# Chunked attention and a gated FFN on one core: heads paired as neighbours, one transfer per weight part, copied rows by a 32-bit or, and a new load order

## The chip, the cores and the metric

The kernel runs on one core of a Trainium2 chip. The metric is the device time of one execution in microseconds (us). Before the change its median is 240.51 us over 3 runs (240.17 to 240.85).

## The reference

Attention over chunks of 32 rows. Each chunk sees 16 rows to its left, itself, 8 rows to its right and 8 memory rows. Its output feeds an FFN with a relu gate. All inputs are f32, with B=4 batches, H=8 heads, S=768 rows and D=64.

```python
for c in range(S // 32):                      # 24 chunks
    l_start, r_end = max(0, 32 * c - 16), min(S, 32 * c + 32 + 8)
    k_full = concat([mem_k, k[:, :, l_start:r_end]], axis=2)      # 8 memory rows + up to 56
    v_full = concat([mem_v, v[:, :, l_start:r_end]], axis=2)
    scores = q[:, :, 32*c:32*c+32] @ k_full.T / sqrt(64)
    a = exp(scores - max(scores));  a = a / (sum(a) + 1e-9)
    out[:, :, 32*c:32*c+32] = a @ v_full
x = out.transpose(0, 2, 1, 3).reshape(3072, 512)
return (relu(x @ w_gate) * (x @ w_val)) @ w_out   # 512 -> 1536 -> 512
```

## The kernel before

**Tiles.** The 3072 tokens are 24 tiles of 128 rows (NT), six for each batch (TPB). A tile holds four chunks. Attention works tile by tile, and the FFN works on blocks of three or four tiles (BLOCKS).

**Attention of a tile.** GpSimd (POOL) loads Q and K with a cast to bf16: `qk_p` holds a pair of tiles (L218, the first six tiles), `qk_b` one tile (L209). TensorE (PE) transposes them into `qk_ps` (L229, L262). ACT or DVE copies the result to `qT` (`pair_q_copy`, L231) and `kT` (`pair_k_copy`, L235). `mem_keys` (L248) puts the transposed memory keys into `kT`, between each chunk's left context and the rest. `scores` (L297) computes 64 scores for each row and head. DVE takes the maximum (`mx`, L310), subtracts it (`dif`, L317), sums the exponents (L329), takes the reciprocal and multiplies (`p_n`, L340). ACT makes the exponents `p_exp` in three key ranges (L325). PE transposes `p_n` (`pT_ps`, L346), which is copied to `pT`. The products with V give `xT_ps` (L363), which is copied to `xT`, the input of the FFN. From tile 14 or 15 on the transposes are done by DMA.

**V.** `v_bd` has two buffers, used by the batches in turn. Each is a block diagonal of two heads: partitions 0 to 63 hold the 64 keys of one head, partitions 64 to 127 those of the other, each head with its own 64 columns. The two heads of a pair are h and h+4 (`HP * par + hp`). The eight memory rows of V must be in `v_bd`, and the off-diagonal part must be zero. For batch 0 both come from a pattern: `vmem_0` holds the memory rows of one chunk, and `pattern_spread` (L177) copies it over all 24 chunks on DVE. For later batches `mem_rows` (L155, its copies at L163) copies them from `vmem` on DVE. `load_v_rows` (L184, issued at L187) loads V itself: in batch 0 in halves of 12 chunks for each pair and parity, later in four loads for a batch. `zero` (L132) clears the second buffer by memset on POOL.

**FFN.** For each block and each of 12 column parts, four products with `w_gate_sb` (`g_ps`, L409), four with `w_val_sb` (`v_ps`, L409), a relu on ACT (`g_relu`, L415) and a multiplication on DVE (`gvT`, L421). The second matrix then takes 12 products for each tile (`out_ps`, L430), with a copy on ACT and a store by SyncE (SP). The gate and value weights come in five groups of columns (WB). Each group is four transfers: two matrices, by the two halves of 64 partitions (`load_gate_val`, L118).

**Order.** The kernel writes its own order. `op()` names a step with the engines that may do it, a cost, what it needs and a priority. `load()` names a POOL issue. `schedule()` runs a model of the engines with these costs: whenever an engine is free, it takes the first ready step by priority. The string LOADS is the order of POOL's issues: K0 and Q0 are pair loads, i the identity, v00 to v13 halves of V of batch 0 (half, pair), w0 to w4 groups of weights, z memsets of the second V buffer, k and q single tiles, o the halves of `w_out`, m the memory values, b the later batches of V. At most eight loads are in flight in the model. LEAD says how far the attention of a block runs ahead of the FFN. Until the first FFN product, PE fills time that it would wait with products on the identity (`idle_ps`, L401).

The order of the first products is by groups of columns over the early blocks, so that each group of weights is used by every early block before the next is needed:

```python
seq = [(blk, m) for g in range(WG) for blk in range(n_early) for m in range(WB[g], WB[g + 1])]
```

Of the kernel before, what the change touches and what calls it, by code (L numbers as in the profile page):

```python
# [12 lines left out]
BF16 = mybir.dt.bfloat16  # L13

# [6 lines left out]
def kernel(  # L21
# [20 lines left out]
    CH = 32  # L42
# [9 lines left out]
    BLOCKS = [3, 3, 4, 4, 3, 3, 4]  # L52
    LEAD = [21, 11, -1, 5, 8, 2, 14, 23]
# [4 lines left out]
    PAIRS = 3  # L58
    MEM_BY_SP = 0
# [3 lines left out]
    LOADS = """Q0 K0 K1 i Q1 K2 Q2 v00 z0 v02 v03 v01 w0 w1 v13 v11 v12 v10 w2 k8  # L63
               k10 w3 q7 k7 k6 q6 w4 q8 q9 k9 z3 o1 z2 z1 o0 m b1 k11 q16 q10
               k15 k12 k14 q11 k23 q21 q12 k16 q13 k13 q14 k20 q23 q15 k21 k19 b2 k17 k18 q17
               q20 q19 q18 q22 k22 b3"""
# [87 lines left out]

    def mem_rows(b, par, hp, eng):  # L155
        p = slice(64 * par, 64 * par + NMEM)
        src = vmem[p, b, HP * par + hp]
        i = bass.AP(tensor=src.tensor, offset=src.offset, ap=[src.ap[0], [0, NCH], [1, D]])
        o = v_bd[b % NSET][p, hp, :, D * par:D * par + D]
        if eng is nc.sync:  # L160
            eng.dma_start(o, i)
        else:
            eng.tensor_copy(o, i)  # L163

    def pattern_load():
        for par in range(2):
            p = 64 * par
            nc.sync.dma_start(
                vmem_f[p:p + NMEM, :, D * par:D * par + D],
                bass.AP(tensor=mem_v.tensor, offset=mem_v[0, HP * par, 0, 0].offset,  # L170
                        ap=[[D, NMEM], [NMEM * D, HP], [1, D]]))
# [12 lines left out]
    def load_v_rows(b, par, s0, s1, c0, c1):  # L184

        dst = v_bd[b % NSET].rearrange("p h c d -> p (h c) d")
        nc.gpsimd.dma_start(  # L187
            dst[64 * par + NMEM + s0:64 * par + NMEM + s1, c0:c1, D * par:D * par + D],
            bass.AP(tensor=v.tensor, offset=v[b, HP * par, 0, 0].offset + (CH * c0 + s0 - 16) * D,
                    ap=[[D, s1 - s0], [CH * D, c1 - c0], [1, D]]))  # L190

    def v_parts(b, par, c0, c1):
        parts = []
        if (b, par, c0) == (0, 0, 0):
            parts.append((b, par, 16, CTX, 0, 1))
            c0 = 1
        if (b, par, c1) == (B - 1, 1, HP * NCH):
            c1 -= 1
            parts.append((b, par, 0, 48, c1, c1 + 1))
        return parts + [(b, par, 0, CTX, c0, c1)]  # L200
# [34 lines left out]
    def pair_k_copy(r, j, eng):  # L235
        b, t = divmod(2 * r, TPB)
        ps = TMP["pair", r, 1]
        o = kT[b][:, :, 4 * t:4 * t + 8, :]
        copy(eng,
             bass.AP(tensor=o.tensor, offset=o.offset + j,  # L240
                     ap=[o.ap[0], [NCH * KW, HP], [KW, 8], [16 + NMEM, 2], [2, 8]]),
             ps[:, j].rearrange("p h (c x s) -> p h c x s", c=8, x=2))
# [5 lines left out]
    def mem_keys(b, eng):  # L248
        src = kmemT[:, b]
        copy(  # L250
            eng, kT[b][:, :, :, 16:16 + NMEM],
            bass.AP(tensor=src.tensor, offset=src.offset,
                    ap=[src.ap[0], [NMEM, HP], [0, NCH], [1, NMEM]]))
# [31 lines left out]
    def scores(a):  # L285
# [3 lines left out]
        for h2 in range(HP):  # L289
            m, par = h2 % 2, h2 // 2  # L290
            for g in range(4):
                c = 4 * t + g
                lo, hi = max(KW * c - 16, 0), min(KW * c + 48, NCH * KW)
                o0 = 64 * (2 * m + par) + lo - (KW * c - 16)
# [17 lines left out]
    def subtract(a):  # L312
# [146 lines left out]
    def psum(n):  # L459
# [9 lines left out]
       prio=(-8,), after=["warm"])  # L469
# [11 lines left out]
    for hp in range(HP):  # L481
        op(("spread", hp), {"DVE": 0.88}, lambda e, hp=hp: pattern_spread(hp), [("vm0", 0), ("vm0", 1)], prio=(-3 + 0.1 * hp,))
    for b in range(B):
        op(("kv", b), {"PE": 0.01}, lambda e, b=b: new_batch(b), take=["kv"],
           prio=(-5.5,) if b == 0 else (1, TPB * b - 2, 0), after=[("t", TPB * b - 2, 0)] if b else [])
        op(("new", b), {"ACT": 0.75}, lambda e, b=b: mem_keys(b, engine[e]), ["kmc", ("kv", b)],
           prio=(-4.5,) if b == 0 else (1, TPB * b - 2, 0))
# [9 lines left out]
    def keys_of(a):  # L497
        return ("tc", a - a % 2 + 1 if a < 2 * PAIRS else a, 1)

    for a in range(NT):  # L500
        b, t = divmod(a, TPB)
        last = t == TPB - 1
        for i in (1, 0):
            if a < 2 * PAIRS:
# [4 lines left out]
                if i:  # L509
                    for j in range(2):  # L510
                        op(("tc", a + j, i), {"ACT": 0.64, "DVE": 0.64}, lambda e, a=a, j=j: pair_k_copy(a // 2, j, engine[e]),
                           [("tc", a, i) if j else ("t", a, i)], (1, a - i, j), (), ["aps"] * j)
                else:
                    op(("tc", a, i), {"ACT": 1.2, "DVE": 1.22}, lambda e, a=a: pair_q_copy(a // 2, engine[e]), [("t", a, i)],
                       (1, a, 0), (), ["aps"])
# [14 lines left out]
           [("tc", a - a % 2 if a < 2 * PAIRS else a, 0), keys_of(a), ("new", b)] + ([] if last else [keys_of(a + 1)]), (1, a, 1), ["sps"],  # L530
           ["kv"] if last else [], ([("s", a - 1)] if a else []) + (pace(a) if a >= BY_DMA[0] else []))
# [16 lines left out]
        ready = [("vl", b, 0 if b else t // 3, n) for n in range(4 if b else 2 * HP)]  # L548
# [19 lines left out]
    for rank, (blk, m) in enumerate(seq):  # L568
        n = BLOCKS[blk]
        if m is not None:  # L570
            for w in range(2):
                op(("f", blk, m, w), {"PE": NFC * (0.0533 * n + 0.0025)}, lambda e, blk=blk, m=m, w=w: first(blk, m, w),
                   [("x", starts[blk] + i) for i in range(n)] + [("w", group_of[m], w, par) for par in range(2)],
# [26 lines left out]
    def load_qk_op(a, i):  # L600
        load(("qk", a, i), 1024, 1.05, lambda: load_qk(a, i), take=["qk"])

    def load_pair_op(r, i):
        load(("qk2", r, i), 1024, 1.66, lambda: load_pair(r, i), take=["pr"])

    def load_v_op(b, half, par, c0, c1, n, deps, after):
        for i, part in enumerate(reversed(v_parts(b, par, c0, c1))):
            rows = part[3] - part[2]
            load(("vl", b, half, n) if i == 0 else ("vx", b, n), rows * (part[5] - part[4]),
                 rows * (part[5] - part[4]) * 1.15e-3, lambda part=part: load_v_rows(*part), deps, (), after)  # L610

    def load_v_half(half, hps):
        c = NCH // 2
        for hp in hps:
            for par in range(2):
                load_v_op(0, half, par, NCH * hp + c * half, NCH * hp + c * half + c, 2 * hp + par, [("spread", hp)], [])

    def load_w_op(g):
        for w in range(2):
            for par in range(2):  # L620
                load(("w", g, w, par), 256, 0.1 + 0.31 * (WB[g + 1] - WB[g]), lambda g=g, w=w, par=par: load_gate_val(g, w, par))
# [4 lines left out]
    def load_batch(b):  # L626
        deps = [("z", x) for x in range(HP)] if b < NSET else [("v", TPB * (b - NSET + 1) - 1)]
        for par in range(2):
            for hp in range(HP):
                if b <= MEM_BY_SP:  # L630
                    op(("mr", b, par, hp), {"SP": 0.73}, lambda e, b=b, par=par, hp=hp: mem_rows(b, par, hp, nc.sync),
                       deps + [(("vm", par), 0.2)], (0, par, hp))
                else:
                    op(("mr", b, par, hp), {"DVE": 0.48}, lambda e, b=b, par=par, hp=hp: mem_rows(b, par, hp, nc.vector),
                       deps + [("vm", par)], (1.5,), (), (), [("s", TPB * b - MEM_LEAD[b])])
        c = HP * NCH // 2
        for par in range(2):
            for x in range(2):
                load_v_op(b, 0, par, c * x, c * x + c, 2 * par + x, [], deps)

    def load_by(name):
# [5 lines left out]
        elif what == "i":  # L647
            load("ident", 0, 0.55, lambda: make_identity(nc, ident_h))
        elif what == "v":
            load_v_half(n // 10, [n % 10])  # L650
# [9 lines left out]
        elif what == "b":  # L660
            load_batch(n)
# [11 lines left out]
    def holds_port(key):  # L673
        return key in ("kmb", "ib") or key[0] in ("vm0", "new", "spread", "mr") or (
            key[0] == "tc" and key[2] == 1 and key[1] >= BY_DMA[1])

    def schedule():
# [30 lines left out]
        while len(started) < len(ops) + len(loads):  # L708
# [8 lines left out]
            while moved:  # L717
                moved = False
                for e in ("POOL", "PE", "ACT", "DVE", "SP"):
                    if free[e] > t + 1e-9:  # L720
                        continue
                    if e == "POOL":
# [7 lines left out]
                        if o["n"]:  # L730
# [4 lines left out]
                            done[key] = queue_end + (1.2 if n_load < 8 else 2.4 if n_load < 45 else 6.0 if key[0] == "vl" else 4.0)  # L735
# [84 lines left out]
```

## Time and profile before

| | before |
|---|---|
| median of 3 runs, us | 240.51 (240.17 to 240.85) |
| profiled execution, its own time, us | 240.34 |
| its span, us | 238.6 |
| PE busy in the span | 225.6 (95%) |
| DVE, ACT, POOL busy | 142.6 (60%), 116.3 (49%), 92.3 (39%) |
| granted TensorE clock, mean | 0.998 |
| DMA moved | 27.17 MB, of it 16.61 MB from POOL's queue |

The span is the stretch between the first and the last instruction that the profiler recorded. The execution's own time is 1.74 us more. A line of a group reads: line, engine, operation, out<-in, count, busy time, mean time of one, idle time ahead and what ended it. A line of the chain or of the timeline begins with a start and a duration, in us from the start of the span. Busy shares are means over stages with different limits, so the stages are read by the chain and the timeline.

### The profile page before, as it was taken

The page shows a single profiled execution, that of the slowest core. Times are in us where ns is not written, and L with a number is a line of the kernel's source. Part 1 is how long each engine was busy: PE and PEld are TensorE (multiplying, and loading weights), DVE is VectorE, ACT ScalarE, POOL GpSimd, SP SyncE. Part 2 cuts the span into 40 slices and gives each one's busy share as a digit, 9 for nine tenths or more (in the row PEclk, how much of TensorE's full clock was granted, in tenths as well). Part 3 has the DMA queues.
Part 4 walks back from the last instruction along what each step waited for, and adds up shares of the span by engine and source line. Part 5 has one row for each costly group of instructions (what it writes and reads, how often), then busy time and mean ns, then how long its engine had stood idle before and what let it go on. Part 6 is the DMA issues. An engine that isn't in the chain of part 4 may idle for free.

```text
span 238.6 us, 5900 instructions
## 1 busy us (share of the span) xinstructions
PE 225.6 (95%) x2439; PEld 125.1 (52%) x2439; DVE 142.6 (60%) x258; ACT 116.3 (49%) x249; POOL 92.3 (39%) x106
## 2 busy tenths in 40 slices
PE   0887989999999999999999999999999999999994
PEld 0666656666644655555444544555546664444442
DVE  4589954559999169969876371068977340234300
ACT  3796653446632766475344442456556541333212
POOL 8999996799567869328400000000000000000000
PEclk9999999999999999999999999999999999999999
DMA  6999999999999999999999964302242101200022
GB/s 69 169 129 145 158 152 166 180 150 180 146 140 203 217 190 139 135 140 153 156 199 137 149 51 107 134 4 56 53 139 69 23 3 45 88 0 0 3 88 88
DMA packets 121115, 27.17 MB, mean 114 GB/s; under 512 B 111232, under 2 KB 118144, under 8 KB 121088
## 3 DMA queue, kind: packets, MB, share of 16 engines
q0 software_dynamic: 101344, 16.61, 95.6%
q1 hardware_dynamic: 19744, 10.18, 20.4%
q8 instruction: 19, 0.31, 0.6%
q14 instruction: 8, 0.07, 0.1%
HBM read 33.24 MB, written 6.29 MB: 166 GB/s over the span
## 4 chain that ended last, share of the span: by engine, by line
PE 85%; POOL 11%; DMA 2%; issue 1%; ACT 0%; ACTq 0%; POOLq 0%
PE out_ps L430 26%; PE v_ps L409 25%; PE g_ps L409 25%; POOL v_bd L187 5%; PE xT_ps L363 3%; POOL qk_p L218 3%; DMA v_bd<-in_v_dram 2%; PE s_ps L297 2%; PE qk_ps L262 2%; POOL w_gate_sb L118 1%; POOL w_val_sb L118 1%; PE pT_ps L346 1%; POOL v_bd L132 1%; POOL ident_h masks.py:197 0%; ACT xT L91 0%
## 5 line engine op out<-in xcount | busy, mean ns | idle before, releaser
L421 DVE TENSOR_TENSOR gvT<-v_ps,g_relu 128x384 f16<-128x384 f32 (+1 forms) x84 | 51.3, 613 | 64.1 <-PE v_ps L409 55.9
L409 PE MATMUL g_ps<-xT,w_gate_sb 128*128 128x384 f16 (+1 forms) x336 | 76.1, 349 | 0.0
L409 PE MATMUL v_ps<-xT,w_val_sb 128*128 128x384 f16 (+1 forms) x336 | 76.0, 349 | 0.0
L415 ACT ACTIVATE g_relu<-g_ps 128x384 f16<-128x384 f32 (+1 forms) x84 | 44.7, 534 | 52.3 <-PE g_ps L409 38.2
L430 PE MATMUL out_ps<-w_out_sb,gvT 128*128 128x512 f16 (+2 forms) x300 | 65.5, 371 | 0.0
L409 PEld LDWEIGHTS <-w_gate_sb 128*128 128x128 f16 x336 | 31.8, 98 | 26.7 <-issue 0.2
L409 PEld LDWEIGHTS <-w_val_sb 128*128 128x128 f16 x336 | 31.7, 98 | 26.8
L430 PEld LDWEIGHTS <-gvT 128*128 128x128 f16 x300 | 27.8, 98 | 29.9
L91 ACT COPY o_sb<-out_ps 128x512 f32<-128x512 f32 (+2 forms) x25 | 14.2, 568 | 37.1 <-PE out_ps L430 35.5
L187 POOL DMA_DIRECT2D v_bd<-in_v_dram x30 | 30.3, 1028 | 0.5 <-issue 0.5
L325 ACT ACTIVATE p_exp<-dif 128x64 f16<-128x64 f32 (+2 forms) x72 | 19.5, 335 | 8.6 <-DVE dif L317 8.5
L209 POOL DMA_DIRECT2D qk_b<-in_q_dram x18 | 16.3, 907 | 14.7 <-DMA v_bd<-in_v_dram 4.8
L209 POOL DMA_DIRECT2D qk_b<-in_k_dram x18 | 17.3, 972 | 6.3 <-DMA v_bd<-in_v_dram 1.8
L329 DVE TENSOR_REDUCE sm<-p_exp 128x8 f32<-128x512 f16 x24 | 16.3, 681 | 4.0 <-ACT p_exp L325 3.8
L310 DVE TENSOR_REDUCE mx<-s_ps 128x8 f32<-128x512 f32 x24 | 16.4, 682 | 2.5 <-PE s_ps L297 2.2
L340 DVE TENSOR_TENSOR p_n<-p_exp,rinv 128x512 f16<-128x512 f16 x24 | 16.5, 686 | 0.4
L317 DVE TENSOR_TENSOR dif<-s_ps,mx 128x512 f32<-128x512 f32 x24 | 16.3, 681 | 0.2
L163 DVE COPY v_bd<-vmem 8x1536 f16<-8x1536 f16 x24 | 16.2, 701 | 0.2
L91 ACT CAST xT<-xT_ps 128x512 f16<-128x512 f32 x20 | 11.3, 585 | 9.4 <-PE xT_ps L363 9.4
L363 PEld LDWEIGHTS <-v_bd 128*128 128x128 f16 x384 | 12.4, 96 | 4.5 <-issue 1.4
L363 PE MATMUL xT_ps<-pT,v_bd 128*128 128x32 f16 x384 | 12.8, 177 | 0.9 <-DMA v_bd<-in_v_dram 0.4
L401 PE MATMUL idle_ps<-ident_h 128*128 128x128 f16 x94 | 8.2, 230 | 5.4 <-POOL ident_h masks.py:199 5.4
(46 smaller groups left out, 129.3 us busy)
## 6 DMA issues: line engine op xcount, KB each, us to landing
out_dram<-o_sb SPq DMA_DIRECT2D x23, 256.0 KB, 2.2
v_bd<-in_v_dram POOLq DMA_DIRECT2D x11, 336.0 KB, 13.8
qk_b<-in_k_dram POOLq DMA_DIRECT2D x18, 128.0 KB, 8.9
qk_b<-in_q_dram POOLq DMA_DIRECT2D x18, 128.0 KB, 8.7
w_out_sb<-in_moe_w_out_dram POOLq DMA_DIRECT2D x2, 768.0 KB, 8.6
v_bd<-in_v_dram POOLq DMA_DIRECT2D x15, 84.0 KB, 4.7
qk_p<-in_q_dram POOLq DMA_DIRECT2D x3, 256.0 KB, 5.7
qk_p<-in_k_dram POOLq DMA_DIRECT2D x3, 256.0 KB, 5.5
```

What stands on the lines that cost most here:

```text
L91: nc.scalar.copy(o, i)
L187: nc.gpsimd.dma_start(dst[64 * par + NMEM + s0:64 * par + NMEM + s1, c0:c1, D * par:D * par + D], bass.AP(tensor=v.tensor, offset=v[b, HP ...
L209: nc.gpsimd.dma_start(qk_b[a, i], bass.AP(tensor=x.tensor, offset=x[b, 0, 128 * t, 0].offset, ap=[[D, 128], [S * D, H], [1, D]]))
L310: nc.vector.reduce_max(SM[a, "mx"], s4, axis=AX.X)
L317: nc.vector.tensor_tensor(out=SM[a, "dif"].rearrange("p (m r) a s -> p r m a s", r=2), in0=S_ps.pop(a).rearrange("p r (m a) s -> p r m a s ...
L325: nc.scalar.activation(p[:, :, :, s0:s0 + k1 - k0], dif[:, :, :, k0:k1], ACT.Exp, scale=SCALE)
L340: nc.vector.tensor_tensor(out=P_n[a], in0=SM.pop((a, "p")), in1=rinv_b, op=ALU.mult)
L363: nc.tensor.matmul(ps[:, hp, r], lhsT=v_bd[b % NSET][:, hp, 4 * t + g, :], rhs=x[:, hp, r], start=True, stop=True)
L409: nc.tensor.matmul(ps, lhsT=w[:, f, 128 * m:128 * m + 128], rhs=xTs[blk][:, f, :], start=(f == 0), stop=(f == NFC - 1))
L415: nc.scalar.activation(st["r", m], st.pop((0, m)), ACT.Relu)
L421: nc.vector.tensor_tensor(out=st["gv"][:, m, :], in0=st.pop((1, m)), in1=st.pop(("r", m)), op=ALU.mult)
L430: nc.tensor.matmul(st["o", t, cols], lhsT=st["gv"][:, m, 128 * t:128 * t + 128], rhs=w_out_sb[:, m, slice(*cols)], start=(m == 0), stop=(m ...
```

## The change

Eight edits in one:

1. The two heads of a pair are now neighbours, 2 hp and 2 hp + 1. The row order of the heads in x therefore becomes the natural one, `scores` and `subtract` lose their permutation, and a part of the gate or value weights is one transfer over 128 partitions instead of two over 64.
2. V is loaded by pair and parity in every batch: eight loads for each later batch instead of four.
3. The pattern is copied in halves of 12 chunks, by ACT (f16 copies) or by DVE, which now uses a bitwise or of the source with itself as 32-bit integers. The memory rows of later batches use the same or.
4. The Q copy of a pair is split by tile, the K copy of the first pair into chunks 0 to 4 and 5 to 7, and the memory keys of batch 0 into halves.
5. The memset of the identity goes from POOL to DVE (`im`).
6. The planner no longer counts pattern copies and memory rows among the steps that hold POOL up, and has new costs.
7. BLOCKS has its fours in other places: from 3, 3, 4, 4, 3, 3, 4 to 3, 3, 3, 4, 3, 4, 4.
8. LOADS and LEAD are new. Thirteen further numbers in LEAD place the pattern copies, the second half of the memory keys, and the scores of tiles 2 to 5 behind steps of the tile before (`behind`).

```diff
-    BLOCKS = [3, 3, 4, 4, 3, 3, 4]
-    LEAD = [21, 11, -1, 5, 8, 2, 14, 23]
+    BLOCKS = [3, 3, 3, 4, 3, 4, 4]
+    LEAD = [16, 5, -1, 6, 1, 3, 15, 24, 17, -6, -4, -1, 11, 8, 24, 4, 18, -6, -3, 1, -3]
-    LOADS = """Q0 K0 K1 i Q1 K2 Q2 v00 z0 v02 v03 v01 w0 w1 v13 v11 v12 v10 w2 k8
-               k10 w3 q7 k7 k6 q6 w4 q8 q9 k9 z3 o1 z2 z1 o0 m b1 k11 q16 q10
...
+    LOADS = """K0 Q0 i K1 v01 Q1 Q2 K2 v03 v02 v00 w0 v10 w1 v13 v12 w2 v11 w3 q6
+               m k8 k6 q9 k23 k9 q16 z1 q7 k7 w4 q8 z2 o1 z3 o0 k10 z0 k13 b11
...
-    def load_gate_val(i, which, par):
+    def load_gate_val(i, which):
...
         nc.gpsimd.dma_start(
-            dst[D * par:D * par + D, :, c0:c0 + n],
-            bass.AP(tensor=src.tensor, offset=src[HP * D * par, c0].offset,
-                    ap=[[DFF, D], [D * DFF, NFC], [1, n]]),
+            dst[:, :, c0:c0 + n],
+            bass.AP(tensor=src.tensor, offset=src[0, c0].offset,
+                    ap=[[DFF, 128], [128 * DFF, NFC], [1, n]]),
...
+    def repeat(eng, o, x):
+        n, w = o.shape[1], o.shape[2]
+        if eng is nc.vector:
+            o, x, w = o.bitcast(I32), x.bitcast(I32), w // 2
+        i = bass.AP(tensor=x.tensor, offset=x.offset, ap=[x.ap[0], [0, n], [1, w]])
+        if eng is nc.vector:
+            nc.vector.tensor_tensor(out=o, in0=i, in1=i, op=ALU.bitwise_or)
+        else:
+            copy(eng, o, i)
...
-    def pattern_spread(hp):
-        src = vmem_0[:, hp]
-        nc.vector.tensor_copy(
-            v_bd[0][:, hp],
-            bass.AP(tensor=src.tensor, offset=src.offset,
-                    ap=[src.ap[0], [0, NCH], [1, 2 * D]]))
+    def pattern_spread(hp, half, eng):
+        n = NCH // 2
+        repeat(eng, v_bd[0][:, hp, n * half:n * half + n], vmem_0[:, hp])
...
-    def pair_q_copy(r, eng):
-        b, t = divmod(2 * r, TPB)
-        copy(eng, qT[b][:, :, 128 * t:128 * t + 256].rearrange("p h (s j) -> p j h s", j=2), TMP.pop(("pair", r, 0)))
+    def pair_q_copy(r, x, eng):
+        b, t = divmod(2 * r + x, TPB)
+        copy(eng, qT[b][:, :, 128 * t:128 * t + 128].rearrange("p h (s j) -> p j h s", j=2),
+             TMP["pair", r, 0][:, :, :, 64 * x:64 * x + 64])
...
-        mx_b = bass.AP(tensor=mx.tensor, offset=mx.offset,
-                       ap=[mx.ap[0], [HP, 2], [2, 2], [1, 2], [0, 64]])
-        nc.vector.tensor_tensor(out=SM[a, "dif"].rearrange("p (m r) a s -> p r m a s", r=2),
-                                in0=S_ps.pop(a).rearrange("p r (m a) s -> p r m a s", a=2),
-                                in1=mx_b, op=ALU.subtract)
+                       ap=[mx.ap[0], [HP, 2], [1, HP], [0, 64]])
+        nc.vector.tensor_tensor(out=SM[a, "dif"].rearrange("p h r s -> p r h s"),
+                                in0=S_ps.pop(a), in1=mx_b, op=ALU.subtract)
...
+    op("im", {"DVE": 0.12}, lambda e: nc.vector.memset(ident_h.bitcast(F32), 0.0), prio=(-8.5,), after=["warm"])
...
+            op(("spread", hp, half), {"DVE": 0.87, "ACT": 0.85},
+               lambda e, hp=hp, half=half: pattern_spread(hp, half, engine[e]), [("vm0", 0), ("vm0", 1)],
+               prio=(1, 0.5 * LEAD[8 + 4 * half + hp], -1))
...
+    def k_parts(r):
+        return [(j, c0, c1) for c0, c1 in (((0, 5), (5, 8)) if r < SPLIT else ((0, 8),)) for j in range(2)]
...
+            load(("w", g, w), 512, 0.05 + 0.66 * (WB[g + 1] - WB[g]), lambda g=g, w=w: load_gate_val(g, w))
...
-                    op(("mr", b, par, hp), {"DVE": 0.48}, lambda e, b=b, par=par, hp=hp: mem_rows(b, par, hp, nc.vector),
-                       deps + [("vm", par)], (1.5,), (), (), [("s", TPB * b - MEM_LEAD[b])])
+                op(("mr", b, par, hp), {"DVE": 0.87}, lambda e, b=b, par=par, hp=hp: mem_rows(b, par, hp, nc.vector),
+                   (deps if b >= NSET else [("z", hp)]) + [("vm", par)], (1.5,), (), (), [("s", TPB * b - MEM_LEAD[b])])
...
-        return key in ("kmb", "ib") or key[0] in ("vm0", "new", "spread", "mr") or (
+        return key in ("kmb", "ib") or key[0] in ("vm0", "new") or (
```

In the order of the changed kernel the planner gives three of the eight pattern copies of batch 0 to ACT and five to DVE. Its POOL order in the head is the new LOADS, in which the third group of weights (w2) stands ahead of the last V pair of the second half (v11).

More of the change, by code (lines that the diff above doesn't have):

```diff
@@ L481 @@
     for hp in range(HP):
-        op(("spread", hp), {"DVE": 0.88}, lambda e, hp=hp: pattern_spread(hp), [("vm0", 0), ("vm0", 1)], prio=(-3 + 0.1 * hp,))
+        for half in range(2):
+            op(("spread", hp, half), {"DVE": 0.87, "ACT": 0.85},
+               lambda e, hp=hp, half=half: pattern_spread(hp, half, engine[e]), [("vm0", 0), ("vm0", 1)],
+               prio=(1, 0.5 * LEAD[8 + 4 * half + hp], -1))
     for b in range(B):
@@ L485 @@
            prio=(-5.5,) if b == 0 else (1, TPB * b - 2, 0), after=[("t", TPB * b - 2, 0)] if b else [])
-        op(("new", b), {"ACT": 0.75}, lambda e, b=b: mem_keys(b, engine[e]), ["kmc", ("kv", b)],
-           prio=(-4.5,) if b == 0 else (1, TPB * b - 2, 0))
+        if b:
+            op(("new", b), {"ACT": 0.75}, lambda e, b=b: mem_keys(b, engine[e]), ["kmc", ("kv", b)], prio=(1, TPB * b - 2, 0))
+    for half in range(2):
+        op(("new", 0, half), {"ACT": 0.42}, lambda e, c=NCH // 2 * half: mem_keys(0, engine[e], c, c + NCH // 2),
+           ["kmc", ("kv", 0)], prio=(1, 0.5 * LEAD[16], -1) if half else (-4.5,))
     def pace(a):
@@ L547 @@
         j = a - starts[blk]
-        ready = [("vl", b, 0 if b else t // 3, n) for n in range(4 if b else 2 * HP)]
+        ready = [("vl", b, 0 if b else t // 3, n) for n in range(2 * HP)]
         ready += [("mr", b, par, hp) for par in range(2) for hp in range(HP)] if b else []
@@ L572 @@
                 op(("f", blk, m, w), {"PE": NFC * (0.0533 * n + 0.0025)}, lambda e, blk=blk, m=m, w=w: first(blk, m, w),
-                   [("x", starts[blk] + i) for i in range(n)] + [("w", group_of[m], w, par) for par in range(2)],
+                   [("x", starts[blk] + i) for i in range(n)] + [("w", group_of[m], w)],
                    (2, rank, w), ["fps"], ["xT"] if (m, w) == (NDC - 1, 1) else [],
@@ L600, in load_qk_op, with load_v_op, load_v_half, mem_rows_ops @@
     def load_qk_op(a, i):
-        load(("qk", a, i), 1024, 1.05, lambda: load_qk(a, i), take=["qk"])
+        load(("qk", a, i), 1024, 0.95, lambda: load_qk(a, i), take=["qk"])
     def load_pair_op(r, i):
[L604 to L612, printed above, removed]
+        load(("qk2", r, i), 1024, 1.5, lambda: load_pair(r, i), take=["pr"])
+    def load_v_op(b, half, par, hp, c0, c1, deps, after):
+        n = 2 * hp + par
+        for i, part in enumerate(reversed(v_parts(b, par, hp, c0, c1))):
+            rows = part[4] - part[3]
+            load(("vl", b, half, n) if i == 0 else ("vx", b, n), rows * (part[6] - part[5]),
+                 rows * (part[6] - part[5]) * 0.95e-3, lambda part=part: load_v_rows(*part), deps, (), after)
+    def load_v_half(half, hp):
         c = NCH // 2
-        for hp in hps:
-            for par in range(2):
-                load_v_op(0, half, par, NCH * hp + c * half, NCH * hp + c * half + c, 2 * hp + par, [("spread", hp)], [])
+        for par in range(2):
+            load_v_op(0, half, par, hp, c * half, c * half + c, [("spread", hp, half)], [])
     def load_w_op(g):
         for w in range(2):
-            for par in range(2):
-                load(("w", g, w, par), 256, 0.1 + 0.31 * (WB[g + 1] - WB[g]), lambda g=g, w=w, par=par: load_gate_val(g, w, par))
+            load(("w", g, w), 512, 0.05 + 0.66 * (WB[g + 1] - WB[g]), lambda g=g, w=w: load_gate_val(g, w))
     def load_zero(hp):
         load(("z", hp), 0, 1.4, lambda: zero(nc.gpsimd, v_bd[1], hp))
-    def load_batch(b):
+    def mem_rows_ops(b):
         deps = [("z", x) for x in range(HP)] if b < NSET else [("v", TPB * (b - NSET + 1) - 1)]
@@ L647, in load_by @@
         elif what == "i":
-            load("ident", 0, 0.55, lambda: make_identity(nc, ident_h))
+            load("ident", 0, 0.35, lambda: make_identity(nc, ident_h, nomemset=True), ["im"])
         elif what == "v":
-            load_v_half(n // 10, [n % 10])
+            load_v_half(n // 10, n % 10)
         elif what == "w":
@@ L734, in schedule @@
                             flying.append(load_end)
[L735 removed]
+                            done[key] = queue_end + (1.5 if n_load < 8 else 2.4 if n_load < 35 else 4.0)
                         else:
```

102 lines of the change are left out of this document (54 added, 48 removed).

## The prediction

> **What bounds the kernel now.** I read the page first (busy time, slices, chain by engine), then the chain in order of time, then the timeline of the first 36 us.
>
> ```profile
> PE 225.6 (95%) x2439; PEld 125.1 (52%) x2439; DVE 142.6 (60%) x258; ACT 116.3 (49%) x249; POOL 92.3 (39%) x106
> ...
> PE 85%; POOL 11%; DMA 2%; issue 1%; ACT 0%; ACTq 0%; POOLq 0%
> ```
>
> ```profile
> 24.07 3.85 POOL v_bd L187 x5
> 28.08 4.39 DMA v_bd<-in_v_dram
> 34.46 0.66 PE g_ps L409 x4
> ...
> 224.85 10.40 PE out_ps L430 x60
> ```
>
> From 34.3 us on PE is the chain and never waits. Before that the chain is POOL, which issues the loads one by one, and the last load of V. So the end is: the time of the first FFN product, plus PE's work behind it, plus PE's waits. The timeline gives all three:
>
> ```profile
> 6.25 0.30 ACT L91 CAST kmem_b<-kmem_f 128x128 bf16<-128x128 f32 x1 [3.37 <-DMA kmem_f<-in_mem_k_dram]
> 7.23 0.83 ACT L91 COPY kT<-kmemT 128x768 bf16<-128x768 bf16 x1
> 7.96 1.33 ACT L91 COPY qT<-qk_ps 128x1024 bf16<-128x1024 bf16 x1
> 8.67 0.82 PE L401 MATMUL idle_ps<-ident_h 128*128 128x128 f16 x6
> 11.80 0.17 DVE L306 MEMSET s_ps<- 32x128 f32 x1 [2.86 <-PE s_ps L297]
> 12.56 0.62 PE L401 MATMUL idle_ps<-ident_h 128*128 128x128 f16 x8
> 14.81 0.67 DVE L310 TENSOR_REDUCE mx<-s_ps 128x8 f32<-128x512 f32 x1
> 22.07 0.69 DVE L340 TENSOR_TENSOR p_n<-p_exp,rinv 128x512 f16<-128x512 f16 x1
> 26.13 0.81 PE L409 MATMUL g_ps<-xT,w_gate_sb 128*128 128x384 f16 x4
> 31.81 0.40 PE L346 MATMUL pT_ps<-ident_h,p_n 128*128 128x128 f16 x4
> 32.61 1.03 PE L363 MATMUL xT_ps<-pT,v_bd 128*128 128x32 f16 x32 [0.40 <-DMA v_bd<-in_v_dram]
> 33.91 0.55 PE L363 MATMUL xT_ps<-pT,v_bd 128*128 128x32 f16 x16 [0.27 <-ACT xT L91]
> 34.31 1.64 PE L409 MATMUL g_ps<-xT,w_gate_sb 128*128 128x384 f16 x8
> ```
>
> The first product starts at 26.13 and the last ends at 224.85+10.40 = 235.25: 209.1 us. PE issues nothing in three gaps: 31.63 to 31.81 (the group at 30.98 is four products of 0.65/4), 32.04 to 32.61, and 33.41 to 33.91 (32 small products at about 0.025). That is 1.25, so the work is 207.9. In those gaps no weights were there for the third group of columns: they landed after the V that PE waited for.
>
> **The change, part by part.** BLOCKS holds, before and after, the same four 3s and three 4s, and the last block stays: the work is the same, and so are the 3.35 us between PE's end and the span's (238.6), and the 1.74 to the run's own time (240.34; the median of the runs is 240.51). Only the new order puts one more p transpose, 0.22, behind the first product: 208.1.
>
> *POOL.* The merged weight loads halve 20 issues of 0.67. One of 512 runs lies between the rows for 256 (0.67) and for 672 (V, 0.80): 0.75, so 20 x 0.67 - 10 x 0.75 = 5.9 us less. The identity's memset (0.96, masks.py) goes to DVE, and the first v_bd memset (1.41) behind the head. The V batches become 8 issues of 1344 runs instead of 4 of 2688 (1.40): between 0.80 and 1.40, about 1.0, so +2.4 us per batch, on an engine that is idle after 116 us; I charge nothing. Cost if that cover were gone: 2.4 us in each later batch.
>
> *DMA.* Group 2 of the weights now goes ahead of the last V pair. By the landings of before (last V part 32.48, group 2's last 35.48) that adds 3.0 in front of V. Taken away are the 2.4 of memsets in which POOL fed nothing, and in part the 0.25 per V load by which the first half (0.80 of POOL each) landed slower than the second (0.585 each): 2.0 to 4.0 together. The last V lands at 31.5 to 33.5, group 2 about 1.2 before it. PE needs group 2 complete at about 32.5 and V at about 34: the three gaps should be filled. This is the gain, 1.25 us.
>
> *The head's start.* ACT stands at the memory keys until 6.25, as before (SP is untouched). Behind the 0.30 of the cast it now has two pattern copies of 128x1536, which DVE made before, in front of scores 0. No row has that form. The SBUF copy of 768 elements took 0.83, and the exponent's rows (257, 348 and 402 ns for 64, 192 and 256) rise by 0.76 ns an element: 1.41, or at most 1.66 for twice the row; I take 1.45. Then kmemT 0.27, two half key copies 0.5 each, five chunks of K 0.5, half of Q 0.73 (as K's 512 elements). 6.55 + 2 x 1.45 + 0.27 + 1.0 + 0.5 + 0.73, less 0.1 for each of seven neighbours that overlap (7.96 in 7.23 + 0.83) is 11.25. Before, the main part of scores 0 started at 11.31. The finer copies thus only pay for the pattern copies. DVE's own copy of Q's other half waits for ACT's and stands ahead of the mask write: 12.2 instead of 11.80.
>
> *The softmax.* DVE's mx 1 stood at 14.81. Now DVE first copies a Q half whose transposes stand behind K's (0.64 to 1.04) and ten idle products. These took (0.82-0.31)/5 = 0.10 each at 8.67, and (0.62-0.22)/7 = 0.057 at 12.56: the clock of PE doubled in between. So mx 1 is at 14.7 to 15.7; 15.3. From there to p_n 2 DVE ran without a gap, 7.26; a K half (0.63) is added: 23.2 instead of 22.07. From p_n 2 to the first product it was 4.06, since p's transposes waited for PSUM until 23.36 and the third xT copy stood in DVE's queue until 25.39. In the new order the earlier xT copies are done by then and the third is ACT's. What remains is 0.69 + 0.52 (transposes) + 0.63 (pT) + 0.6 (values) + 0.66 (xT) = 3.1: first product at 26.3, against 26.13.
>
> *DVE later.* The 24 memory row copies (median 549 ns) become 32-bit ors of 768 elements. gvT's rows (690 for 512, 555 for 384 elements) give 1.05 ns an element, so 0.686 + 256 x 1.05 = 0.95. Sixteen of them, +0.4 each, fall where DVE was busy 13.98 of 18.5 us (64 to 82.5): +6.5 against 4.5 free, but the new order starts them in front of 64, where a third is free. Between 0 and 2.0 on PE; I take 0.
>
> *Sum.* 26.3 + 208.1 = 234.4, against 235.25: -0.9. 240.34 - 0.9 = 239.4.
>
> **Rivals.**
> *Late weights (slower).* PE's wait for V becomes one for group 2 or 3 of the weights, which now have 0.2 to 2 us to spare. For: DMA runs at 1.5 to 2 queues deep through the head, and two thirds of the new margin comes from an estimate. Against: half parts landed 0.64 to 0.76 apart, so 1.3 to 1.5 a part. It decides from about 1.7 a part: six parts are then 1.8 later, 0.8 beyond the spare time, and group 3 and w_out, again as tight, cost as much: +2.4, so 241.8.
>
> *DVE becomes the bound (slower).* If an or takes 1.2 (a POOL that is in its way, or a slower 32-bit path), sixteen add 4 more: +2 on PE between 64 and 90, 241.4. Against: p_n's instruction has two SBUF inputs too and took 683 to 694 beside POOL's issues, which stayed at 0.80.
>
> *Cheaper pattern copies (faster).* The change's own cost for ACT's is 0.85. Then scores 0 starts 1.2 earlier and the first product by about 0.9; but the weights are the next late thing, and 0.4 of it is lost: 238.9. Against: every ACT row here has over 0.7 ns an element.
>
> *A slow clock (no change).* In the new order PE has nothing from about 10.3 (its last idle products) to 11.4. If the clock doubles later for that, mx 1 comes at 15.7 and the first product 0.4 later, 26.7: 239.8. [...]
>
> **How the numbers follow.** A measurement of this kernel can tell 0.3%, 0.72 us, from no change: faster is under 239.6. The forecast has 0.45, of which 0.15 falls within 0.3%; cheaper copies 0.25; the slow clock 0.10; late weights 0.13; DVE 0.07. So faster 0.55, same 0.25, slower 0.20. The range reaches from the cheap copies with no loss (238.2) to the late weights (241.9).
>
> **What would show it.** Right: the copies of the pattern on ACT at 1.4 to 1.5 each; mask write of scores 0 at 12.2; first L409 product at 26 to 26.7; no DMA wait on PE from there; V values behind products of group 2. Wrong: ACT copies under 1.0 (then earlier); PE waits for w_gate_sb, w_val_sb or w_out_sb (late weights); ors over 1.1, or PE waiting for gvT or p_n between 54 and 95 (DVE).

## The result, and the profile after

| | before | after |
|---|---|---|
| median of 22 runs each, us | 240.83 (240.10 to 242.99) | 239.59 (239.01 to 240.94) |
| ratio to before | | 0.9942 (95%: 0.9925 to 0.9959) |
| profiled execution, own time, us | 240.34 | 239.73 |
| its span, us | 238.6 | 238.0 |
| first FFN product, last product's end, us | 26.13, 235.25 | 26.67, 234.64 |

The change makes the kernel 0.58% faster (0.41 to 0.75%); 239.4 us was forecast. The two profiled executions differ by only 0.6 us: that of before lies 0.5 us under its median, that of after 0.14 above.

The page after, in the lines that answer to those of before: PE has the same work, and the chain is now PE's with some DVE and ACT; POOL is gone from it.

```profile
PE 225.6 (95%) x2439; PEld 125.7 (53%) x2439; DVE 151.6 (64%) x266; ACT 117.7 (49%) x252; POOL 91.2 (38%) x107
...
PE 89%; DVE 4%; ACT 2%; DMA 2%; SPq 1%; issue 0%; ACTq 0%
```

The timeline of after (start, duration, engine, line, what). In the text, a number behind a step is its tile: scores 0, mx 1, p_n 2.

```profile
3.28 1.47 ACT L93 COPY v_bd<-vmem 128x1536 f16<-128x1536 f16 x1
6.39 0.30 ACT L93 CAST kmem_b<-kmem_f 128x128 bf16<-128x128 f32 x1 [1.64 <-DMA kmem_f<-in_mem_k_dram]
6.60 1.47 ACT L93 COPY v_bd<-vmem 128x1536 f16<-128x1536 f16 x1
8.13 1.47 ACT L93 COPY v_bd<-vmem 128x1536 f16<-128x1536 f16 x1
9.50 1.35 PE L401 MATMUL idle_ps<-ident_h 128*128 128x128 f16 x11
11.48 0.59 PE L298 MATMUL s_ps<-kT,qT 64*32 64x48 bf16 x32 [0.63 <-ACT qT L93]
12.27 0.17 DVE L307 MEMSET s_ps<- 32x128 f32 x1
12.99 1.25 PE L401 MATMUL idle_ps<-ident_h 128*128 128x128 f16 x10
15.76 0.67 DVE L311 TENSOR_REDUCE mx<-s_ps 128x8 f32<-128x512 f32 x1
23.36 0.68 DVE L340 TENSOR_TENSOR p_n<-p_exp,rinv 128x512 f16<-128x512 f16 x1
23.94 0.28 PE L298 MATMUL s_ps<-kT,qT 64*32 64x64 bf16 x24 [0.22 <-issue]
26.67 0.81 PE L409 MATMUL g_ps<-xT,w_gate_sb 128*128 128x384 f16 x4
34.49 0.96 PE L363 MATMUL xT_ps<-pT,v_bd 128*128 128x32 f16 x32
35.29 0.81 PE L409 MATMUL v_ps<-xT,w_val_sb 128*128 128x384 f16 x4
35.94 0.56 PE L363 MATMUL xT_ps<-pT,v_bd 128*128 128x32 f16 x16
```

Two things are to be read here. Behind 26.67 PE waits for nothing: the values of tiles 3 to 5 stand behind products of group 2 and between others, and from the first product to the end it is 234.64 - 26.67 = 207.97, against 209.12 before. That is 1.15 us gained. Ahead of 26.67 the head has become longer by 0.54. The difference, 0.61, is what the two profiles show. Against a second profile of before (m8, below) it is 0.81.

### The profile page after: what moved, and what is told of

Its sections match the earlier page's. It is cut to its first block, busy times and chain, and to the rows that moved or that the text cites. A ratio compares the mean times of both kernels' runs of the same rounds, so it can differ in the third digit from the quotient of the medians.

```text
span 238.0 us, 5900 instructions
## 1 busy us (share of the span) xinstructions
PE 225.6 (95%) x2439; PEld 125.7 (53%) x2439; DVE 151.6 (64%) x266; ACT 117.7 (49%) x252; POOL 91.2 (38%) x107
## 4 chain that ended last, share of the span: by engine, by line
PE 89%; DVE 4%; ACT 2%; DMA 2%; SPq 1%; issue 0%; ACTq 0%
PE v_ps L409 27%; PE out_ps L430 26%; PE g_ps L409 26%; PE xT_ps L363 3%; PE s_ps L298 2%; DMA kmem_f<-in_mem_k_dram 2%; PE qk_ps L264 2%; ACT v_bd L93 1%; PE pT_ps L346 1%; DVE mx L311 1%; DVE dif L318 1%; DVE sm L329 1%; PE qk_ps L230 1%; PE idle_ps L401 1%; DVE p_n L340 1%; ACT kT L93 1%
## 5 line engine op out<-in xcount | busy, mean ns | idle before, releaser
L188 POOL DMA_DIRECT2D v_bd<-in_v_dram x42 | 37.6, 917 | 21.0 <-PE xT_ps L363 13.7
L409 PEld LDWEIGHTS <-w_val_sb 128*128 128x128 f16 x336 | 31.4, 98 | 26.5
L163 DVE TENSOR_TENSOR v_bd<-vmem 8x768 int32<-8x768 int32 (+1 forms) x29 | 26.6, 940 | 0.2
L210 POOL DMA_DIRECT2D qk_b<-in_k_dram x18 | 16.2, 901 | 4.0 <-DMA w_val_sb<-in_moe_w_val_dram 1.5
L363 PEld LDWEIGHTS <-v_bd 128*128 128x128 f16 x384 | 12.6, 96 | 4.0 <-issue 0.3
L93 ACT CAST xT<-xT_ps 128x512 f16<-128x512 f32 x16 | 9.3, 586 | 6.0 <-PE xT_ps L363 5.7
L298 PE MATMUL s_ps<-kT,qT 64*32 64x64 bf16 (+2 forms) x768 | 8.1, 194 | 1.5 <-ACT qT L93 0.6
```

Of the source, the lines that this page charges most:

```text
L93: nc.scalar.copy(o, i)
L163: nc.vector.tensor_tensor(out=o, in0=i, in1=i, op=ALU.bitwise_or)
L188: nc.gpsimd.dma_start(v_bd[b % NSET][64 * par + NMEM + s0:64 * par + NMEM + s1, hp, c0:c1, D * par:D * par + D], bass.AP(tensor=v.tensor, ...
L210: nc.gpsimd.dma_start(qk_b[a, i], bass.AP(tensor=x.tensor, offset=x[b, 0, 128 * t, 0].offset, ap=[[D, 128], [S * D, H], [1, D]]))
L363: nc.tensor.matmul(ps[:, hp, r], lhsT=v_bd[b % NSET][:, hp, 4 * t + g, :], rhs=x[:, hp, r], start=True, stop=True)
L409: nc.tensor.matmul(ps, lhsT=w[:, f, 128 * m:128 * m + 128], rhs=xTs[blk][:, f, :], start=(f == 0), stop=(f == NFC - 1))
```

## The experiments

The ratio is always to the kernel before; the runs are named m1 to m12. "A" and "B" are the two theories on the gain behind the first product: the new order (A), or the saved POOL issues (B).

**Edits 1 and 2 alone (m1).** `load_gate_val` gives one transfer for `par == 0` and none for `par == 1`, heads are 2 hp and 2 hp + 1, V of later batches goes by pair; the rest is the kernel before.

```diff
-            dst[D * par:D * par + D, :, c0:c0 + n],
+            dst[:, :, c0:c0 + n],
...
-        src = vmem[p, b, HP * par + hp]
+        src = vmem[p, b, 2 * hp + par]
```

> The kernel before with edits 1 and 2 alone: heads paired as neighbours, each weight part in one transfer, V of later batches in eight transfers. Every other engine keeps the order of before; LOADS, BLOCKS and the head are those of before. Theory A (the gain comes from group 2 of the weights standing ahead of the last V pair; V and weights are limited by moving the data, not by POOL's issues): four weight parts less to issue in front of the last V brings V only about 0.4 us earlier, nothing else fills the gap, so the end moves by 0.3 to 0.5: ratio to before about 0.998. Theory B (the saved issues alone are the gain): 8 issues of 0.67 become 4 of 0.78 ahead of the last V, 2.2 us; V lands at about 30.3 instead of 32.48, the three gaps (1.25 us) close: 0.995. Both: first FFN product at 26.1 as before.

Measured: 0.9985 (0.9969 to 1.0). POOL does finish issuing sooner, but only until it meets another limit. Its last two V loads of the head wait until earlier weight transfers have landed:

```profile
26.04 0.78 POOL L190 DMA_DIRECT2D v_bd<-in_v_dram  x1 [0.66 <-DMA w_gate_sb<-in_moe_w_gate_dram]
27.45 0.78 POOL L190 DMA_DIRECT2D v_bd<-in_v_dram  x1 [0.63 <-DMA w_val_sb<-in_moe_w_val_dram]
```

So the last V landed at 31.86, 0.62 earlier than the 32.48 of before, not 2.2 earlier. B's size is wrong. By the ratio the merged transfers alone give about a quarter of the gain. This profile gives about half: from the first FFN product to the end of the last it has 208.6 us, against 209.1 before and 208.0 in the changed kernel. PE no longer waits for V there, but 0.26 for a copy of `pT`.

**The order of group 2 alone (m2).**

```diff
-  ... w0 w1 v13 v11 v12 v10 w2 k8
+  ... w0 w1 v13 v11 w2 v12 v10 k8
```

> The kernel before with one edit in LOADS: w2 goes from behind v10 to ahead of v12, so four transfers of group 2 stand in front of the last two V pairs; the planner moves PE's products of group 2 ahead of the values of tile 3 accordingly. Weight parts stay in two transfers. Theory A (the order is what gains): PE has products of group 2 where it waited for V, the gaps (1.25 us) close: ratio 0.995 to 0.997. Theory B (the order without the saved issues only moves the wait): the last V lands some 3 us later than 32.48, at about 35, PE waits for it about 1 us after the extra products, and the xT copies still leave 0.5 to 1.2: end 0.5 to 1.0 later than before, ratio 1.002 to 1.004.

Measured: 1.0029 (1.0005 to 1.0053), slower, as B had it. In the waits of PE behind its first product:

```profile
PE g_ps L409 <- ACT xT L91: 0.7, 1, 0.7
PE xT_ps L363 <- DMA v_bd<-in_v_dram: 0.5, 1, 0.5
PE xT_ps L363 <- ACT xT L91: 0.3, 1, 0.3
PE v_ps L409 <- DMA w_val_sb<-in_moe_w_val_dram: 0.2, 1, 0.2
```

The last V now lands at 35.47, 3.0 later, as B had it; PE waits for it again, for group 2, and for copies of `xT` with no product left to put between. The order by itself costs; A alone falls.

**The changed kernel with two transfers per weight part (m3).**

```diff
+        for p in (0, 64):
             nc.gpsimd.dma_start(
-                dst[:, :, c0:c0 + n], ...
+                dst[p:p + 64, :, c0:c0 + n], ...
```

> The changed kernel with each weight part in two transfers of 64 partitions again (20 issues instead of 10), every engine's order kept. Theory A (the order carries the gain): group 2 still stands ahead of the last V pair, and as the data are what limits the landings, the end is within 0.7 us of the changed kernel: ratio to before 0.994 to 0.997. Theory B (the saved issues are needed): six extra issues of about 0.55 in front of the last V, 3.3 us on POOL; group 2 lands at 32 to 34 instead of 29.8 and 30.9, PE waits for w_gate_sb, w_val_sb or v_bd for 1.0 to 2.0 us: ratio 0.998 to 1.002.

Measured: 0.9992 (0.9968 to 1.0016): no gain is left that shows. In its timeline the wait for V is back:

```profile
35.16 0.88 PE L364 MATMUL xT_ps<-pT,v_bd 128*128 128x32 f16 x28 [0.55 <-DMA v_bd<-in_v_dram]
```

The last V landed at 35.02 instead of 32.22, 2.8 later for six extra issues. Together with the two runs above, by the ratios: merged parts alone gain 0.36 us, the order alone loses 0.7, the whole change gains 1.4 and loses 1.2 of it again without the merged parts. From the first FFN product to the end the profiles have 208.6, 210.1, 208.0 and 208.8, against 209.1 before. The order needs the saved issues, and it is the order that turns the larger part of them into time.

**16-bit copies in place of the or (m4).**

```diff
-            o, x, w = o.bitcast(I32), x.bitcast(I32), w // 2
...
-            nc.vector.tensor_tensor(out=o, in0=i, in1=i, op=ALU.bitwise_or)
+        copy(eng, o, i)
```

> The changed kernel with every or of DVE (five pattern copies, 24 memory row copies) as a copy of 16-bit elements again, order kept. Theory A (the form of these copies does not reach the end): each copy takes 0.55 to 0.75 instead of 0.94, POOL's issues beside the pattern copies rise from 0.91 to 1.2 to 1.6, the last V lands up to 1 us later than 32.22, inside the 2.3 us that it has to spare before PE's values at 34.49: within 0.3% of the changed kernel, ratio to before 0.993 to 0.996. Rival C (DVE, busy 18.20 of 18.5 us between 64 and 82.5, is the bound there): the copies free 24 x 0.3 us and the end moves forward by 0.7 us or more: below 0.991. Rival D (POOL's issues beside them hold up the head): slower by 0.5 to 1.5 us: 0.996 to 1.000.

Measured: 0.9943 (0.9918 to 0.9967), the same as the changed kernel. The median of these copies is 0.544 us against 0.943, and between 64 and 82.5 us DVE is busy 13.68 instead of 18.20 (first line: changed kernel, second: this one; stretch, then the busy time of PE, PEld, DVE, ACT and POOL, the granted clock and the DMA):

```profile
64.00:82.50 18.50, 18.50 (x178) 9.86 (x177) 18.20 (x27) 9.21 (x20) 14.17 (x17) 1.00 2.17 188
64.00:82.50 18.50, 18.50 (x192) 10.19 (x191) 13.68 (x25) 9.80 (x21) 14.91 (x17) 1.00 2.14 193
```

PE is busy all the time in both. C and D fall: the or moves the end by less than these runs can show, 0.6 us. The profile is of this kernel's fastest execution (238.75, median 239.47).

**The gap on PE ahead of scores 0 filled (m5).**

```diff
+    order[at(("s", 0)):at(("s", 0))] = [(0.0, idle_product, None)] * 7
```

> The changed kernel with seven more idle products on PE ahead of scores 0, where PE had nothing from 10.65 to 11.48; all else and every other order kept. [...] Rival F (the clock doubles at a moment that PE's gap has nothing to do with): the same as the changed kernel, 0.994, and the seven products delay scores 0 by up to 0.1.

Measured: 0.9955 (0.993 to 0.9979), no better than the changed kernel, whose ratio F has. In this profile PE's steps halve at 12.2, and mx 1 stands at 14.60 instead of 15.76. Then PE loses what that gained, with idle time that ended by nothing that another engine did (`<-issue`, below "a stall by issue"):

```profile
14.60 0.67 DVE L311 TENSOR_REDUCE mx<-s_ps 128x8 f32<-128x512 f32 x1
18.26 0.21 PE L298 MATMUL s_ps<-kT,qT 64*32 64x64 bf16 x5 [1.45 <-issue]
25.06 0.31 PE L298 MATMUL s_ps<-kT,qT 64*32 64x64 bf16 x31 [0.73 <-issue]
27.85 0.33 PE L409 MATMUL g_ps<-xT,w_gate_sb 128*128 128x384 f16 x1
```

Both stalls are in the middle of one row of score products, which depend on nothing new. Between 10 and 30 us the trace has three transfers on the instruction queue, of 16 KB each. In the trace of the changed kernel one starts at 21.58, 2.36 us ahead of PE's going on at 23.94, behind its stall of 0.22. Behind the first stall of m5 the steps of the 24 idle products are 0.107 again (2.71 us for all of them, 1.51 in the changed kernel): PE had also lost its clock, whose mean over this execution is 0.993.

This profile is of one of the slower executions (240.90, median 239.78). Six of the twelve have a mean granted clock of 0.991 to 0.993, as this one has, and took 239.94 to 241.85. The other six have 1.0 and took 239.33 to 239.62, no better than the changed kernel's median. A lost clock thus goes with the slower half; what holds up the other half no profile shows.

**Two pattern copies out of ACT's way (m6), and the same with group 2 moved further ahead (m7).**

```diff
+    move(("spread", 3, 1), "kmb", "ACT")
+    move(("spread", 0, 1), ("kc", 0, 2), "DVE")
...
+        x, y = place["w", 2, w], place["vl", 0, 1, 4 + w]
+        x["swap"], y["swap"] = y["fn"], x["fn"]
```

The second copy goes ahead of the memory keys' cast, the third becomes an or on DVE. The last two lines are in m7 alone: w2 and v12 change places in POOL's order.

> The changed kernel with two of ACT's three pattern copies (1.47 us each) out of the way of scores 0: the second goes ahead of the memory keys' cast, into the time that ACT waits for their load (4.75 to 6.39), the third becomes an or on DVE, which is idle from 9.43 to 10.87. Theory G (these copies delay scores 0): scores 0 start at 10.4 to 10.7 instead of 11.48 without a gap on PE in front, mx 1 at 14.1 to 14.7, the first FFN product at 25.0 to 25.6. What limits the end then: if only the head (theory H), the end is 1.1 to 1.5 earlier than in the changed kernel: ratio to before 0.988 to 0.9895. If the landings of group 2 (30.9) and of the last V pair (32.2) come in its way, being bound by the data that DMA moves (theory A), PE waits 0.5 to 1.0 for w_gate_sb, w_val_sb or v_bd and the end is only 0.5 to 0.8 earlier: 0.991 to 0.992.

> The kernel of the run above with group 2 of the weights also ahead of the V pair before the last (w2 and v12 exchanged in POOL's order, PE's order kept). Theory A (landings bound by data): group 2 lands 1.2 earlier, at 28.5 and 29.7, no wait for it is left, but the last V pair still lands at 32.2 and group 3 at 34.1 to 36: PE waits 0.5 to 1.0 there instead, and the time is that of the run above within 0.3%: 0.990 to 0.992. Theory H': the wait for group 2 was the only one: 0.988 to 0.9895.

Measured: 0.9916 (0.9891 to 0.9941) and 0.9916 (0.9887 to 0.9945). The numbers are A's, but A's reason is not there: in neither profile does PE wait for weights or V. In the first:

```profile
10.68 0.62 PE L298 MATMUL s_ps<-kT,qT 64*32 64x48 bf16 x32
17.49 0.58 PE L230 MATMUL qk_ps<-ident_b,qk_p 128*64 128x128 bf16 x14 [0.92 <-issue]
23.28 0.28 PE L298 MATMUL s_ps<-kT,qT 64*32 64x64 bf16 x24 [0.86 <-issue]
26.01 0.81 PE L409 MATMUL g_ps<-xT,w_gate_sb 128*128 128x384 f16 x4
```

Scores 0 start 0.8 earlier and mx 1 stands at 14.18, as G has it, but the first product comes only 0.66 earlier: two stalls by issue of 1.78 together. In the second (one stall of 0.47) it comes at 25.43; that is m7's fastest execution (238.49, median 239.14). Three of m7's six have the full clock and took 238.49 to 238.75, the other three 0.993 and 239.53 to 239.91. In every kernel built on the changed one with merged parts (m4 to m7 and m9 to m11) PE's last product ends 207.96 behind the first FFN product, whether that is at 24.73 or 27.85: in these profiles the landings never bind, and only the head counts. An execution's own time is then the first product plus 213.06.

**The kernel before again (m8).**

> The kernel before, unchanged, for a second profile. The profiles of before and of the changed kernel differ by 0.6 us in their spans, the medians of the runs by more than 1 us. If executions of before differ in when the last V pair lands and when PE's clock doubles, this profile shows a last V landing other than 32.48 by 0.3 us or more, PE's wait for v_bd (0.40 then) other by as much, and the doubling at another moment than 12.4; the first FFN product stays within 0.5 of 26.13. If not, all three are the same within 0.1 and the difference of the medians stays unexplained.

Measured: 240.55 us, span 238.8. The first product is at 26.02; PE stands 0.71 instead of 0.40 ahead of the values of tile 3, with the last V landing at 32.67 (32.48), and its steps halve between 10.6 and 11.7 (12.2 to 12.6). The view names ACT's copy of `pT` for this wait, but that one started 0.11 sooner than in the first profile, and V landed 0.14 ahead of the products (0.13). Executions of before do differ so; V is 0.19 later, less than the 0.3 expected.

**Idle products four in a row as one of 512 columns**, in the changed kernel (m9), in m5 (m10) and in m7 (m11).

```diff
-        nc.tensor.matmul(TMP["idle"], lhsT=ident_h, rhs=ident_h, start=True, stop=True)
+            TMP["idle"] = fps.tile([128, 512], F32, tag="fps", name="idle_ps")
+        x = ident_h[:, 0:128]
+        x = bass.AP(tensor=x.tensor, offset=x.offset, ap=[x.ap[0], [0, n], [1, 128]])
...
```

`x` is the identity repeated n times by a step of 0, with n up to 4.

> The changed kernel in which up to four idle products in a row are one product of 512 columns: the same time on PE with about 70 products and as many weight loads fewer in PE's program, all else in the same order. Theory I (PE's own instructions arrive in blocks of 16 KB, some 2.4 us after the transfer of a block starts in the trace, and a dense row of small instructions empties PE's supply): the idle time that ends by issue in the middle of scores 4 (0.22 in the changed kernel, 0.86 and 0.73 in the two kernels where PE was earlier) and the 0.20 in the transposes at 18.25 go: first FFN product 0.2 to 0.5 earlier than 26.67, or 25.4 to 25.7 where the clock doubles before 13.5: ratio 0.991 to 0.9935. Without theory I: no difference, 0.994 to 0.9945.

> The kernel of m5 (seven more idle products in PE's gap ahead of scores 0), with up to four idle products in a row as one of 512 columns. Theory I: m5 lost the gain of its earlier clock to two stalls by issue of 1.45 and 0.73 us; here neither is above 0.3, mx 1 stays at 14.5 to 15.1, the first FFN product comes at 25.5 to 26.0 and the end at 233.5 to 234.0: ratio 0.990 to 0.992 (m5: 0.9955). Rival J (m5's stalls are of another cause than the number of PE's instructions, or of that one execution): ratio as m5, 0.994 to 0.996, stalls of 0.7 and more again.

> The kernel of m7 (two pattern copies out of ACT's way, group 2 ahead of two V pairs), with up to four idle products in a row as one of 512 columns. Theory I: the first FFN product comes at 24.9 to 25.4 with no stall by issue above 0.3 before it. Then the landings decide: the last V at 32.2 to 32.5 and group 3 at 34.1 to 36.5 are bound by the data that DMA moves, and PE waits 0 to 0.8 for v_bd or the weights: end at 233.0 to 233.5, ratio 0.988 to 0.9905 (m7: 0.9916). Rival J: as m7, 0.991 to 0.992, with a stall of 0.3 to 0.9 in scores 4.

Measured: 0.9876 (0.9837 to 0.9915), 0.9882 (0.9847 to 0.9918) and 0.9864 (0.9827 to 0.9901). By the ratios each is faster than its parent by 0.5 to 0.7%, by the medians alone by 0.4 to 0.5%, and in the first two the intervals do not touch the parent's. None of the 19 executions has a granted clock under 0.997, so the lost clock of m5 and m7 is a part of the difference: m7 with the full clock took 238.49 to 238.75, and m11's median is 238.27. In m10 the two stalls of m5, 2.18 together, have become one, larger than the 0.3 expected:

```profile
25.25 0.30 PE L298 MATMUL s_ps<-kT,qT 64*32 64x64 bf16 x29 [0.47 <-issue]
25.61 0.81 PE L412 MATMUL g_ps<-xT,w_gate_sb 128*128 128x384 f16 x4
```

In m11 there is none, and its first product is at 24.73:

```profile
10.81 0.62 PE L298 MATMUL s_ps<-kT,qT 64*32 64x48 bf16 x32
24.26 0.31 PE L298 MATMUL s_ps<-kT,qT 64*32 64x64 bf16 x32
24.73 0.81 PE L412 MATMUL g_ps<-xT,w_gate_sb 128*128 128x384 f16 x4
```

It is the fastest kernel here: 238.27 us median, 1.36% under before by the ratio. The profile of m9 is of its slowest execution (240.62, median 238.41) and cannot show where its typical one gains; that execution has a stall by issue of 0.79 in scores 5, where the changed kernel has 0.22 in scores 4. J's ratios fall, for m10 and for m11.

**Wide idle products in the kernel before (m12).**

> The kernel before, with up to four idle products in a row as one of 512 columns, all else in the same order. Theory K (only the changed order is so dense at its start that PE's supply of instructions runs out; before, PE's idle time ahead of the first FFN product is ended by DVE and ACT, not by issue, in both of its profiles): nothing changes, the first FFN product stays at 26.0 to 26.2: ratio 0.998 to 1.001. Rival L (fewer idle products help any order alike, as they did in the changed kernel, by 0.6 to 0.7%): 0.993 to 0.995.

Measured: 1.005 (1.0026 to 1.0074). L falls, but K's "no change" does too: it is slower. The profile is that of its fastest execution (240.66, median 242.0), with the first product at 26.34 and no stall by issue ahead of it, so it does not show the loss. The cause of the loss stays open, and that the last three gains come from the supply of instructions is not shown.

## Why the prediction was right, and where it was off

- *The gain, 1.25 us behind the first product.* Right, 1.15 in the profiles. The work was put at 208.1 and is 207.97; the last V was put at 31.5 to 33.5 and landed at 32.22, group 2 about 1.2 before it and 1.33 before it. That the whole of it takes both the order and the saved issues is shown by the three runs that have only one.
- *POOL.* 0.75 for a merged weight issue; the medians are 0.77 and 0.79.
- *Pattern copies on ACT.* 1.45; measured 1.47. That they only eat up what the finer copies bring: right for the start of scores 0 (qT done at 11.43, 11.25 forecast; mask write 12.27, 12.2 forecast).
- *The step that failed: the clock behind the head.* mx 1 was put at 15.3 with idle products at 0.057 from about the same time as before. In the profile it stood at 15.76, the ten idle products at 12.99 still took 0.11 each, and the first product came at 26.67 instead of 26.3. That is the rival "a slow clock" almost to the digit (15.7, 26.7, 239.8; that execution took 239.73). It was given 0.10, and it fits this execution. The median execution, 239.59, had its first product at about 26.5 (an estimate: 239.59 less 213.06). The 16-bit kernel, with the same order on PE, had the fast step at 9.9 and its first product at 25.70 in its fastest execution. The forecast, with the clock of before, lay between two cases of which neither has that moment.
- *Tail of the head.* p_n 2 to the first product: 3.1 forecast, 3.31 measured, of it 0.22 the stall by issue, which the working did not have.
- *DVE later.* 0.95 an or, 0.94 measured; DVE 18.20 of 18.5 us busy, and PE without a wait: the 0 that was taken of 0 to 2.0.
- *Late weights.* The spare time was larger than feared (group 2 complete at 30.89, needed at 33.19). The run with split parts shows the case: 0.55 of waiting, 1.2 us in all.
- *The total.* 0.9 of gain was forecast on the profiled execution (235.25 less 234.4 is 0.85); 0.6 in the two profiles, 1.2 between medians. The sum was made against an execution of before that was 0.5 faster than its median. That 239.4 came within 0.2 of the median is in part luck: in the profile the head came 0.37 later than forecast, and the work behind it was 0.13 shorter.

The small edits (BLOCKS, the split Q and K copies, the identity's memset) were not tried alone, so what each is worth is not shown. One of them ends a wait in the profile after: the 0.63 ahead of scores 0 ends with a half copy of Q on ACT.

## What to carry to other kernels

Saved issues on a queue are worth only what the order behind them makes of them: here the merged loads alone gave 0.36 us and the order alone lost 0.7, and together they gave 1.4. Where a head decides and the rest is fixed (207.96 in every kernel with the whole change), look at what the path engine is made to do while it waits: fillers cost instructions too, and the same PE time in about a quarter of the fillers' instructions took 1 us off the changed kernel (238.41 against 239.59 by the medians), but slowed the one before (1.005). Sum against several executions where one step (a clock, a landing) differs from one to the next.

## What the runs showed of the hardware

**The moment at which PE's clock doubles differs from execution to execution.** The steps of idle products go from 0.107 to 0.056 at this moment; the trace's record of the full clock begins at 12.47 in before and at 14.78 in after. m8 is the same kernel as before, and its steps halve between 10.6 and 11.7. The five profiles in which PE was idle from 10.5 or 10.8 to 11.45 (m4, m10, after, m3, m9) doubled at 9.9, 9.9, 14.8, 15.2 and 16.6; of those without that gap, before, m5, m6, m7, m8, m11 and m12 doubled between 10.8 and 13.1. So the gap stands with the two earliest moments and with the three latest, and in m4 and m10 the doubling came ahead of it: that the gap makes it later, as the rival "a slow clock" had it, is not shown. Filling the gap moved no median (m5 beside after, m10 beside m9), so how often each case occurs stays open.

**PE stood still in the middle of rows of products and transposes that wait for nothing the trace shows.** The page of after counts the transfers on the instruction queue:

```profile
q8 instruction: 19, 0.31, 0.5%
```

That is 19 of 16 KB, as in before. Of the six profiles with the changed order and the clock doubled by 13.1, five have 0.47 to 2.18 us of stalls by issue in the head (m7 and m10 the least, m5 the most; m11 has none). With the later clock m9 has 0.79, after 0.22 and m3 none. The steps differ: scores 2 or the transposes behind them, and scores 4, or scores 5 with wide idle products. None of the profiles with the head of before (before, m1, m2, m8, m12) has one. The scores of one tile are 32 products and as many weight loads in 0.31 us (scores 1 of after). With wide idle products the stalls went from 2.18 to 0.47 (m5, m10) and from 0.47 to none (m7, m11), but from 0.22 to 0.79 in the profiles of after and m9. That PE's instructions came too late there is theory I, the author's estimate; no profile shows it by itself. An early clock and a shorter head thus came together with stalls: in their profiles m6's first product was 0.66 earlier, half of what G expected, with stalls of 1.78, and m5's 1.18 later, with stalls of 2.18 and the lost clock.
